# One transfer instead of two for the tokens of a block, and another order of ScalarE's conversions, in a Fourier and two-layer kernel on Trainium2

## The chip, the cores and the metric

The kernel runs on 1 core of one Trainium2 chip. The metric is the device time of one execution in microseconds (us). Engines are named as in the profile: PE (matmul), PEld (its weight loads), DVE (VectorE), ACT (ScalarE), POOL (GpSimd), SP (SyncE, which here only issues transfers).

## What is computed

Three stages follow each other (shapes: batch 4, sequence 3072, width 256):

```python
X = np.fft.fft(np.fft.fft(x, axis=1), axis=2).real          # Fourier stage, (4, 3072, 256)
h = X @ moe_w_in                                             # width 2048
y = np.where(h > 0, h, np.exp(np.minimum(h, 0)) - 1) @ moe_w_out
h = np.maximum(y @ moe2_w_in, 0); u, v = h[..., :512], h[..., 512:]
vn = (v - mean(v)) / sqrt(var(v) + 1e-6)
out = (u * (einsum('ts,bsd->btd', w_spatial, vn) + b)) @ moe2_w_out
```

## The kernel before, in words

The order of work on every engine is the order of the program text; only semaphores hold an engine back. Float32 products are made of three matmuls of a high and a low part (`matmul3`, L186 to L191), so most operands are split into two tiles: ACT rounds (`copy`, L164), then DVE or POOL subtracts (L165).

**Fourier stage** (L239 to L480). Twelve slots (four batches, three parts of the sequence) of folding on DVE and matmuls on PE. Its results are written to DRAM as `a` (16 blocks of 128 x 2 x 384 or 386, one for each batch b and token class c) by `evac` (L357); ACT copies them out of PSUM, and for the last batch ACT also issues the store. Beside this, weights that arrive as 64-bit floats are converted to float32: `late_load(n)` (POOL issues a transfer of 512 KB into a tile `wbits`), `late_begin(n)` (two passes on ACT: `mag`, and `cvr`, the rest), `late_end(n)` (six operations on DVE, which also issues the load of n + 2) and `late_keep(n)` (POOL issues a store of `cvr` into the tile `big`). Twelve such weights are converted in all: 0 to 4 at the end of the Fourier stage, 5 and 6 while `moe_w_in` is multiplied by the Fourier matrix (`pw`, L535 to L557), the rest in the first steps of the next stage. Two `wbits` tiles and a few `cv` tiles are used in turn, so a conversion can wait for an earlier one's store.

**Middle stage** (L567 to L840), both layers of the first perceptron and the first of the second. The 16 blocks of tokens follow each other, with eight steps each (a step is two of the sixteen slices of the 2048 units). A step s runs `s1` (the slice's products `pe` and `po`), `combine` on DVE, an ELU on ACT and DVE, and three steps later `s2`, which accumulates the second product in four PSUM banks `acc`. After the last step of a block `evac_x2` splits the four banks, and 14 *pieces* are put on a list: six `v_piece` (normalised on POOL and DVE, stored by SP and added up in DRAM by accumulating POOL transfers `v<-v`) and eight `u_piece` (L740). They run one or two at a time in the next block's steps: the last two `u` pieces at the end of step 7, the first `v` and `u` of the new list at the start of the step after it. A `u_piece` is six matmuls into a PSUM bank `pu`, a ReLU on ACT into one of three SBUF tiles in turn (L754, L755), and a store to DRAM that SP issues (L756); ACT can write a tile again only when its store three pieces ago has landed. The banks of `pe`, `po`, `pv`, `pu` are four in turn.

The tokens of a block are loaded by `load_x` (L501): half 0 of `a` (128 rows of 1536 or 1544 bytes, L504), half 1 without its row 0 (127 rows, L505), and row 0 of the middle column, broadcast to 128 rows (`xmid`, L508). Row 0 of half 1 must be zero: POOL clears it once before the first block (L523), and as the tile `xraw` is one and the same, no load touches that row. `split_x` (L511) rounds on ACT and subtracts on POOL. In the main loop the load for the block after the next step group is issued at the end of step g = 1 (L836, from block 1 on), and split at g = 4.

**Last stage** (from L842), the product with the 3072 x 3072 matrix, 1400 us, not touched.

Of the kernel before, what the change touches and what calls it, by code (L numbers as in the profile page):

```python
# [9 lines left out]
F32 = mybir.dt.float32  # L10
F32R = mybir.dt.float32r
U32 = mybir.dt.uint32
# [3 lines left out]
P = 128  # L16
B, S, D = 4, 3072, 256
# [5 lines left out]
TC = 512  # L23
NCH = S // TC
ND = 129
EVE = 386
# [36 lines left out]
def chunk_n(c):  # L63
    return EVE if c == 0 else ODD
# [67 lines left out]
def fourier_ffn_gated_kernel(ctx: ExitStack, tc: tile.TileContext, t, out: bass.AP):  # L132
    nc = tc.nc
# [28 lines left out]
    def split(hi, lo, src, engine=None):  # L162

        nc.scalar.copy(hi, src)  # L164
        (engine or nc.vector).tensor_tensor(lo, src, hi.bitcast(F32), op=ALU.subtract)  # L165
# [30 lines left out]
    late_at, late_raw, late_weights = {}, {}, []  # L196
    EARLY = 5

    def late_load(n):
        if n < len(late):  # L200
            name, at, _ = late[n]
            late_at[n] = [wr.tile([P, 2, D, 2], U32, tag="bits", bufs=2, name="wbits")]
            nc.gpsimd.dma_start(late_at[n][0], t[name][at])

    def late_begin(n, mag=None):
# [6 lines left out]
    def late_end(n, **k):  # L212
        if n < len(late):
            bits, mag = late_at.pop(n)
            num = wr.tile([P, 2 * D], U32, tag="cv1", name="cv1")
            f64_end(late_raw[n], bits.rearrange("p a d w -> p (a d) w"), mag, num, late_raw[n], **k)
            late_load(n + 2)

    def late_halves(n):
        _, at, dst = late[n]  # L220
# [18 lines left out]
    with ExitStack() as ph:  # L239
# [21 lines left out]
        def load_q(b, i):  # L261
            if b not in qs:
                home, tag = (big_p, f"big{b - 1}") if b in (1, 2) else (qp, "q")
                qs[b] = home.tile([P, 3, 4, 4, ND], F32, tag=tag, name=f"q{b}")
            nc.sync.dma_start(qs[b][:, i], t["xq"][b, :, i])
# [137 lines left out]
        load_bits(2)  # L403
        load_rows384(1)
        load_q(1, 0)
        def load_dt():
            nc.sync.dma_start(raw_dt, t["dt"])

# [9 lines left out]
        for k in range(SLOTS):  # L418
            b, i = divmod(k, 3)
            if done and (k in PACE or k == SLOTS - 1):  # L420
                w1_high(done - 1)
            fold(b, i)
            if i == 0:
                row0(b)
            mid_columns(b, i)
            if b and i == 0:
                for c in CLASSES:
                    evac(b - 1, c)
            if i == 2:
                keep_mids(b)  # L430
            for c in CLASSES:
                for z in range(2):
                    group(b, c, z, i)
            if k in PACE:
                if done:
                    w1_low(done - 1)
                else:
                    w1_begin(0)
                w1_end(done)
                load_bits(done + 3)  # L440
                done += 1
                w1_begin(done)
            for f, *a in loads.get(k, []):
                f(*a)
            if k == SLOTS - 1:
                w1_low(done - 1)
            if k == 4:
                nc.scalar.copy(halves_dt, raw_dt)
            if k == SLOTS - 3:
                late_load(0)  # L450
                late_load(1)
                big = [big_p.tile([P, 12 * TC], F32R, tag=f"big{x}", name=f"big{x}") for x in range(2)]
                late_weights.append([x[:, : NF1 * D].rearrange("p (f d) -> p f d", f=NF1) for x in big])
            if k == SLOTS - 2:
                late_begin(0, cvp.tile([P, TC], U32, tag="mag", name="mag"))

        row_sums = {}
        mid_rows = xop.tile([B, 2, EVE], F32, tag="mid_rows", bufs=1, name="mid_rows")

# [5 lines left out]
        def evac_rows(c):  # L465
# [1 line left out]
            nc.scalar.dma_start(m_d[c], mid_rows[:, c, : chunk_n(c)])  # L467

        beside = {
            0: [(evac, B - 1, 2)],  # L470
            1: [(evac, B - 1, 3)],
            2: [(sum_rows, 0), (evac, B - 1, 0), (evac, B - 1, 1), (sum_rows, 1)],
            3: [(evac_rows, 0), (evac_rows, 1)],
        }
        for n in range(EARLY):
            late_end(n)
            late_keep(n)
            late_begin(n + 1, cvp.tile([P, TC], U32, tag="mag", name="mag") if n < EARLY - 1 else None)
            for f, *a in beside.get(n, []):
                f(*a)  # L480

# [10 lines left out]
    wo1, weo = late_weights[0], [[x[:, NF1 * D :] for x in big], [wp.tile([P, DFF1], F32R, name=f"wo{h}") for h in "hl"]]  # L492
    wmid = wp.tile([P, NF1], F32, name="wmid")

    nh = vp.tile([P, 1], F32, name="nh", bufs=1)
    nc.gpsimd.memset(nh, -0.5)

    blocks = [(b, c) for b in range(B) for c in range(4)]
    xt = {}

    def load_x(i):  # L501
        b, c = blocks[i]
        n = chunk_n(c)
        nc.sync.dma_start(xraw[:, 0, :n], a_d[b][c][:, 0])  # L504
        nc.sync.dma_start(xraw[1:, 1, :n], a_d[b][c][1:, 1])  # L505
        m = xp.tile([P, EVE], F32, tag="xmid", bufs=2, name=f"xmid{i}")
        src = m_d[c][b] if c < 2 else a_d[b][c][0, 1]
        nc.sync.dma_start(m[:, :n], src.partition_broadcast(P))  # L508
        xt[i] = m

    def split_x(i):  # L511
        m = xt[i]
        n = chunk_n(blocks[i][1])
        hi = xp.tile([P, 2, EVE], F32R, tag="xhi", bufs=2, name=f"xhi{i}")
        lo = xp.tile([P, 2, EVE], F32R, tag="xlo", bufs=2, name=f"xlo{i}")
        split(hi[:, :, :n], lo[:, :, :n], xraw[:, :, :n], nc.gpsimd if i else None)
        xt[i] = (hi, lo, m)

    def load_wmid(q):
        nc.sync.dma_start(wmid[:, 4 * q : 4 * q + 4], wm_d[q].rearrange("o (f p) -> p (o f)", p=P))  # L520

    xraw = xp.tile([P, 2, EVE], F32, tag="xraw", name="xraw")
    nc.gpsimd.memset(xraw[:1, 1], 0.0)  # L523
    load_x(0)
    split_x(0)
    load_x(1)
    with tc.tile_pool(name="w1p", bufs=2, reuse_waits="tile", side="right") as w1p:
        row = None

        def mid_row(q, acc):  # L530
            x = w1p.tile([1, TC], F32, tag="mid_row", name="mid_row")
            nc.scalar.copy(x, acc[:1])
            nc.scalar.dma_start(wm_d[q], x)

        for q in range(DFF1 // TC):  # L535
            s = slice(q * TC, (q + 1) * TC)
            pieces = [w1_piece(2 * q + kt) for kt in range(2)]
            sums = [pp.tile([P, TC], F32, tag="pp", name=f"pw{z}") for z in range(2)]
            for z in range(2):
                for kt in range(2):  # L540
                    matmul3(
                        sums[z],
                        [x[:, kt, z * P : (z + 1) * P] for x in dt],
                        pieces[kt],
                        kt == 0,
                        kt == 1,
                    )
            for z in range(2):
                split(*(x[:, s] for x in weo[z]), sums[z])
            if row is not None:  # L550
                mid_row(*row)
            row = q, sums[1]
            if q % 2 == 0:
                n = EARLY + q // 2
                late_end(n)
                late_keep(n)
                late_begin(n + 1)  # L557
        mid_row(*row)
# [217 lines left out]
    def run_norms(n=None):  # L776
# [7 lines left out]
            nm()  # L784
        del norms[:n]

    NG = len(groups)
    LAG = 3
    PIECES = (2, 2, 2, 2, 1, 2, 1, 2)
    for s in range(NG + LAG):  # L790
        new = s < NG
        tail = s - LAG
        step = groups[tail][1] if tail >= 0 else -1
        if 0 <= s - 2 < NG:
            dve_g(s - 2)
        if 0 <= s - 1 < NG:
            act_neg(s - 1)
        if new:
            pe, po = s1(s, 0)
            combine(s, 0, pe, po)  # L800
        n = s + EARLY
        late_low(n - 1)
        late_end(n)
        late_keep(n)
        if step == 0:
            run_pieces(PIECES[0])
        if tail >= 0:
            s2(tail, 0)
        if new and groups[s][0] == 1:
            split_wo1(groups[s][1])  # L810
        if 0 <= s - 2 < NG and not plain(s - 2):
            act_hi(s - 2)
            dve_lo(s - 2)
        if 0 <= s - 1 < NG:
            act_exp(s - 1)
        late_begin(n + 1)
        late_high(n)
        if new:
            pe, po = s1(s, 1)
            combine(s, 1, pe, po)  # L820
        run_norms()
        run_sums(2)
        if tail >= 0:
            s2(tail, 1)
        if step == 7:
            evac_x2(groups[tail][0])
        if 1 <= step <= 7:
            run_pieces(PIECES[step])
        if step == 7:
            i = groups[tail][0]  # L830
            u = [("u", i, j, h) for j in range(4) for h in range(2)]
            for k in range(6):
                pieces += [("v", i, k), u.pop(0)]
            pieces += u
        if new and groups[s][0] < len(blocks) - 1:
            if groups[s][1] == 1 and groups[s][0]:  # L836
                load_x(groups[s][0] + 1)
            if groups[s][1] == 4:
                split_x(groups[s][0] + 1)
    ffn_early.close()  # L840
# [390 lines left out]
```

## Time and profile before

| | |
|---|---|
| median of 3 runs | 2814.07 us (2811.02 to 2817.68) |
| the profiled execution | 2814.41 us, span 2812.6 us |
| busy share of the span | PE 96%, PEld 83%, DVE 74%, ACT 46%, POOL 18% |
| mean granted TensorE clock | 0.979 of full |
| middle stage, 280 to 1235 us: PE busy | 874.4 of 955 us |

The span runs from the first to the last instruction of the program; the execution's own time is 1.8 us more. Busy shares are means over three stages with different limits, so the stretches are to be read one by one. A clock of 1.00 is 2.4 GHz, 0.50 is 1.2 GHz.

### The profile page before, as it was taken

How to read it: one execution, taken by the hardware profiler on the slowest of the kernel's cores; microseconds unless marked ns; L12 is line 12 of the kernel's file. 1: busy time of each engine (PE TensorE's matmuls, PEld its weight loads, DVE VectorE, ACT ScalarE, POOL GpSimd, SP SyncE). 2: the span in 40 equal slices, each digit the busy share in tenths (PEclk: the TensorE clock that was granted, in tenths of full speed). 3: DMA queues.
4: the chain of work that ended last, by engine and by line, in shares of the span. 5: the costliest groups of instructions: out<-in, count | busy, mean ns of one | idle time of the engine just before them, and what ended most of it. 6: DMA issues, size and time to landing. Idle time of an engine off the chain costs nothing.

```text
span 2812.6 us, 34540 instructions
## 1 busy us (share of the span) xinstructions
PE 2686.9 (96%) x12588; PEld 2328.8 (83%) x12588; DVE 2072.2 (74%) x2541; ACT 1288.8 (46%) x1709; POOL 495.5 (18%) x909
## 2 busy tenths in 40 slices
PE   8889989988889999989899999999999999999999
PEld 4559989988879899989788888888888888888877
DVE  9799777777777787777577766776966577676775
ACT  3457666666656667666332332323333233322332
POOL 0102233343441243434202010000000000000000
PEclk9999999999999999999999999999999999999999
DMA  9412465556664565656969789787856777677683
GB/s 375 141 35 108 132 128 142 126 129 132 122 118 159 141 142 136 125 121 139 292 239 334 251 274 302 252 279 251 308 209 236 246 260 254 232 266 276 225 288 111
DMA packets 212654, 565.01 MB, mean 201 GB/s; under 512 B 24952, under 2 KB 50553, under 8 KB 210948
## 3 DMA queue, kind: packets, MB, share of 16 engines
q1 hardware_dynamic: 165598, 460.53, 46.1%
q0 software_dynamic: 45888, 100.68, 19.4%
q8 instruction: 98, 1.61, 0.2%
q10 hardware_dynamic: 998, 1.61, 0.2%
q14 instruction: 72, 0.59, 0.1%
HBM read 397.01 MB, written 171.48 MB: 202 GB/s over the span
## 4 chain that ended last, share of the span: by engine, by line
PE 80%; DVE 8%; DMA 5%; ACT 3%; SPq 1%; issue 1%; POOL 0%; DVEq 0%; ACTq 0%; POOLq 0%
PE a L190 17%; PE a L191 17%; PE a L189 17%; PE acc L189 5%; PE acc L191 4%; PE acc L190 4%; DMA u<-uu 4%; PE pa L345 2%; DVE glo L637 2%; PE po L189 1%; PE pv L189 1%; PE pv L190 1%; PE po L190 1%; PE po L191 1%; PE pv L191 1%
## 5 line engine op out<-in xcount | busy, mean ns | idle before, releaser
L191 PE MATMUL a<-whi,vlo 128*128 128x512 f32 x1920 | 747.5, 389 | 0.0
L190 PE MATMUL a<-wlo,vhi 128*128 128x512 f32 x1920 | 747.3, 389 | 0.0
L189 PE MATMUL a<-whi,vhi 128*128 128x512 f32 x1920 | 747.0, 389 | 0.0
L910 ACT CAST whi<-raw 128x1024 fp32r<-128x1024 f32 x240 | 252.5, 1053 | 808.8 <-PE a L191 415.9
L916 DVE TENSOR_TENSOR wlo<-raw,whi 128x1024 fp32r<-128x1024 f32 x240 | 293.7, 1224 | 369.0 <-ACT whi L910 368.8
L190 PEld LDWEIGHTS a<-wlo,vhi 128*128 128x128 f32 x1920 | 360.4, 188 | 75.3
L189 PEld LDWEIGHTS a<-whi,vhi 128*128 128x128 f32 x1920 | 360.4, 188 | 75.2
L191 PEld LDWEIGHTS a<-whi,vlo 128*128 128x128 f32 x1920 | 360.3, 188 | 75.0
L637 DVE TENSOR_TENSOR glo<-h,ghi 128x1536 fp32r<-128x1536 f32 (+1 forms) x120 | 224.2, 1869 | 228.4 <-ACT ghi L632 228.4
L189 PE MATMUL acc<-ghi,big 128*128 128x384 f32 (+1 forms) x960 | 333.7, 348 | 0.0
L191 PE MATMUL acc<-ghi,big 128*128 128x384 f32 (+1 forms) x960 | 331.9, 346 | 0.0
L190 PE MATMUL acc<-glo,big 128*128 128x384 f32 (+1 forms) x960 | 331.2, 345 | 0.0
L900 DVE TENSOR_TENSOR raw<-raw 128x1024 f32<-128x1024 f32 x240 | 294.2, 1226 | 10.9 <-DMA raw<-in_wT 7.6
L955 POOL DMA_DIRECT2D u<-u x32 | 25.7, 834 | 1112.0 <-DVE sum L972 668.8
L608 ACT ACTIVATE e<-h 128x1536 f32<-128x1536 f32 (+1 forms) x128 | 190.0, 1484 | 55.0 <-DVE h L600 55.0
L773 POOL DMA_DIRECT2D v<-v x226 | 203.2, 1262 | 49.9 <-DVE v L727 37.4
L622 DVE SCALAR_TENSOR_TENSOR h<-e,h 128x1536 f32<-128x1536 f32 (+1 forms) x120 | 210.4, 1753 | 0.0
L613 ACT ACTIVATE e<-e 128x1536 f32<-128x1536 f32 (+1 forms) x128 | 190.4, 1487 | 0.2
L190 PEld LDWEIGHTS acc<-glo,big 128*128 128x128 f32 x960 | 188.0, 196 | 0.2
L189 PEld LDWEIGHTS acc<-ghi,big 128*128 128x128 f32 x960 | 187.5, 195 | 0.1
L191 PEld LDWEIGHTS acc<-ghi,big 128*128 128x128 f32 x960 | 186.8, 195 | 0.0
L632 ACT CAST ghi<-h 128x1536 fp32r<-128x1536 f32 (+1 forms) x120 | 176.3, 1469 | 21.5 <-DVE h L622 21.2
(166 smaller groups left out, 4183.2 us busy)
## 6 DMA issues: line engine op xcount, KB each, us to landing
raw<-in_wT SPq DMA_DIRECT2D x480, 512.0 KB
vlo<-v SPq DMA_DIRECT2D x120, 512.0 KB
v<-v POOLq DMA_DIRECT2D x226, 256.0 KB, 5.9
v<-v SPq DMA_DIRECT2D x224, 256.0 KB
u<-uu SPq DMA_DIRECT2D x128, 192.0 KB
u<-u POOLq DMA_DIRECT2D x16, 1024.0 KB, 8.6
q<-in_xq SPq DMA_DIRECT2D x12, 1032.0 KB
out<-sum SPq DMA_DIRECT2D x48, 256.0 KB
```

The source lines that it names most:

```text
L189: nc.tensor.matmul(acc, lhsT=w[0], rhs=x[0], start=start, stop=False, skip_group_check=more)
L190: nc.tensor.matmul(acc, lhsT=w[0], rhs=x[1], start=False, stop=False, skip_group_check=more)
L191: nc.tensor.matmul(acc, lhsT=w[1], rhs=x[0], start=False, stop=stop, skip_group_check=more)
L608: nc.scalar.activation(e[:, :, :w], st[s]["h"][:, :, :w], AF.Relu, scale=-1.0)
L613: nc.scalar.activation(e[:, :, :w], e[:, :, :w], AF.Exp, scale=-1.0)
L622: nc.vector.scalar_tensor_tensor(out=g[:, :, :w], in0=e[:, :, :w], scalar=-1.0, in1=h[:, :, :w], op0=ALU.add, op1=ALU.max)
L632: nc.scalar.copy(st[s]["hi"][:, :, :w], st[s]["h"][:, :, :w])
L637: nc.vector.tensor_tensor(st[s]["lo"][:, :, :w], st[s]["h"][:, :, :w], st[s]["hi"][:, :, :w].bitcast(F32), op=ALU.subtract)
L773: nc.gpsimd.dma_start(dst, v, accum_op=ALU.add)
L900: nc.vector.tensor_tensor(res, total, y, op=ALU.add if sg > 0 else ALU.subtract)
L910: nc.scalar.copy(hi, total)
L916: nc.vector.tensor_tensor(lo, total, hi.bitcast(F32), op=ALU.subtract)
```

## The change

`load_x` takes a new tile for each block and loads both halves of `a` with one transfer of 128 rows. A new `clear_x` lets POOL set row 0 of half 1 to zero behind the load, before `split_x`; in the main loop it stands at the end of step g = 2. At the end of the Fourier stage weights 2 and 3 are loaded into the three `bits` tiles of the pool `cvp` earlier (their loads no longer wait for `late_end(0)` and `late_end(1)`, which now load 4 and 5), and ACT's conversions stand elsewhere in its order: 1 and 2 ahead of the last batch's copies, 3 and 4 between them, 5 behind the rounding of the first `pw`. The tile `nh` is allocated and set later.

```diff
-    def late_load(n):
+    def late_load(n, home=wr, bufs=2):
...
-            late_load(n + 2)
+            if n not in (2, 3):
+                late_load(n + (4 if n < 2 else 2))
...
             if k == SLOTS - 2:
-                late_begin(0, cvp.tile([P, TC], U32, tag="mag", name="mag"))
+                late_load(2, cvp, 3)
+                early_begin(0)
+
+        late_load(3, cvp, 3)
...
         beside = {
-            0: [(evac, B - 1, 2)],
-            1: [(evac, B - 1, 3)],
-            2: [(sum_rows, 0), (evac, B - 1, 0), (evac, B - 1, 1), (sum_rows, 1)],
+            0: [(early_begin, 1), (early_begin, 2), (evac, B - 1, 2)],
+            1: [(evac, B - 1, 3), (early_begin, 3)],
+            2: [(sum_rows, 0), (evac, B - 1, 0), (evac, B - 1, 1), (sum_rows, 1), (early_begin, 4)],
             3: [(evac_rows, 0), (evac_rows, 1)],
         }
         for n in range(EARLY):
             late_end(n)
             late_keep(n)
-            late_begin(n + 1, cvp.tile([P, TC], U32, tag="mag", name="mag") if n < EARLY - 1 else None)
...
-        nc.sync.dma_start(xraw[:, 0, :n], a_d[b][c][:, 0])
-        nc.sync.dma_start(xraw[1:, 1, :n], a_d[b][c][1:, 1])
+        raw = xp.tile([P, 2, EVE], F32, tag="xraw", name=f"xraw{i}")
+        nc.sync.dma_start(raw[:, :, :n], a_d[b][c])
...
+    def clear_x(i):
+        nc.gpsimd.memset(xt[i][0][:1, 1, : chunk_n(blocks[i][1])], 0.0)
...
-    xraw = xp.tile([P, 2, EVE], F32, tag="xraw", name="xraw")
-    nc.gpsimd.memset(xraw[:1, 1], 0.0)
     load_x(0)
+    clear_x(0)
     split_x(0)
...
                 n = EARLY + q // 2
+                if q == 0:
+                    late_begin(n)
                 late_end(n)
...
             if groups[s][1] == 1 and groups[s][0]:
                 load_x(groups[s][0] + 1)
+            if groups[s][1] == 2:
+                clear_x(groups[s][0] + 1)
             if groups[s][1] == 4:
                 split_x(groups[s][0] + 1)
```

## Rows read from the trace of the kernel before

**Rows 1.** The page: busy time of each engine in us, share of the span, instructions.

```profile
PE 2686.9 (96%) x12588; PEld 2328.8 (83%) x12588; DVE 2072.2 (74%) x2541; ACT 1288.8 (46%) x1709; POOL 495.5 (18%) x909
```

**Rows 2.** Stretches: length, busy us of PE, PEld, DVE, ACT, POOL, clock, DMA share, GB/s.

```profile
280.00:1235.00 955.00, 874.40 (x4663) 847.62 (x4662) 722.74 (x930) 621.89 (x843) 345.13 (x647) 0.96 0.58 131
...
908.00:978.00 70.00, 69.17 (x372) 67.29 (x372) 56.77 (x74) 49.23 (x67) 23.30 (x49) 0.98 0.57 142
```

**Rows 3.** Waits, 280 to 1235 us: who for whom, us in all, times, longest.

```profile
ACT uu L755 <- DMA u<-uu: 105.0, 13, 12.6
...
PE po L189 <- ACT uu L755: 77.4, 13, 10.5
```

**Rows 4.** Timeline of SP, 640 to 720 us: start, length, instruction.

```profile
655.12 0.35 SPq L505 DMA_DIRECT2D xraw<-a  x1
655.81 6.07 SPq L508 DMA_DIRECT2D xmid<-m  x1
...
666.80 9.22 SPq L756 DMA_DIRECT2D u<-uu  x3
```

**Rows 5.** Timeline of ACT and PE in the same boundary between blocks.

```profile
661.11 0.49 ACT L755 ACTIVATE uu<-pu 128x384 f32<-128x384 f32 x1 [0.21 <-PE pu L191]
...
675.18 0.49 ACT L755 ACTIVATE uu<-pu 128x384 f32<-128x384 f32 x1 [9.59 <-DMA u<-uu]
...
675.73 0.69 PE L189 MATMUL po<-xhi,woh 128*128 128x384 f32 x1 [7.47 <-ACT uu L755]
```

**Rows 6.** Stretches at that boundary, columns as in the second group.

```profile
656.00:662.00 6.00, 6.00 (x36) 6.00 (x35) 5.79 (x10) 4.86 (x7) 1.77 (x2) 1.00 1.11 222
...
670.00:674.00 4.00, 0.00 (x0) 0.00 (x0) 0.00 (x0) 0.00 (x0) 0.00 (x0) 0.93 0.07 25
```

**Rows 7.** Timeline of SP, 178 to 200 us.

```profile
181.76 0.29 SPq L505 DMA_DIRECT2D xraw<-a  x1
196.59 0.35 SPq L508 DMA_DIRECT2D xmid<-a  x1
```

**Rows 8.** Stretches behind those transfers, columns as in the second group.

```profile
187.00:189.00 2.00, 2.00 (x11) 1.60 (x10) 2.00 (x2) 1.97 (x2) 0.00 (x0) 1.00 0.07 25
...
193.00:196.00 3.00, 3.00 (x13) 2.06 (x12) 2.21 (x5) 1.88 (x2) 0.00 (x0) 1.00 0.00 0
...
198.00:200.00 2.00, 2.00 (x11) 1.60 (x10) 0.86 (x1) 2.00 (x3) 0.00 (x0) 1.00 0.22 68
```

**Rows 9.** Line 505, 270 to 1235 us: ns min/median/max of an issue, first and last start.

```profile
L505 SPq DMA_DIRECT2D xraw<-a x13: 278/344/730, 281.2 to 1189.5; - x13
```

**Rows 10.** Timeline of ACT at the last boundary between blocks.

```profile
1274.01 0.49 ACT L755 ACTIVATE uu<-pu 128x384 f32<-128x384 f32 x1 [0.21 <-PE pu L191]
...
1278.58 0.49 ACT L755 ACTIVATE uu<-pu 128x384 f32<-128x384 f32 x1
```

**Rows 11.** First and last of 13 stretches of 8 us, each from where PE resumes.

```profile
297.00:305.00 8.00, 8.00 (x37) 8.00 (x38) 5.87 (x7) 5.22 (x6) 2.99 (x6) 0.79 0.23 84
...
1210.30:1218.30 8.00, 8.00 (x31) 8.00 (x32) 5.87 (x7) 5.21 (x6) 4.77 (x8) 0.64 0.23 83
```

**Rows 12.** Timeline, end of the Fourier stage; idle time before and its releaser in brackets.

```profile
113.22 0.67 ACT L170 ACTIVATE mag<-wbits 128x512 f32<-128x512 f32 x1 [1.43 <-DMA wbits<-in_moe_w_out]
...
118.37 0.41 POOL L523 MEMSET xraw<- 1x386 f32 x1
...
119.65 0.66 ACT L170 ACTIVATE cv<-wbits 128x512 f32<-128x512 f32 x1 [3.53 <-DMA big<-cvr]
...
120.76 0.83 ACT L164 CAST xhi<-xraw 128x772 fp32r<-128x772 f32 x1
```

**Rows 13.** The chain that ended last, first piece on PE behind it.

```profile
184.69 0.45 PE po L189
```

**Rows 14.** Timeline of POOL behind the load of a block.

```profile
676.47 0.19 POOL L719 TENSOR_SCALAR ve<-sums 128x1 f32<-128x1 f32 x1 [18.69 <-ACT sq L718]
```

**Rows 15.** Transfers issued in 654 to 676 us: times, KB each, median us to landing.

```profile
v<-v POOLq DMA_DIRECT2D x4, 256.0 KB, 8.5
```

More of the change, by code (lines that the diff above doesn't have):

```diff
@@ L197, in fourier_ffn_gated_kernel @@
     EARLY = 5
-    def late_load(n):
+    def late_load(n, home=wr, bufs=2):
         if n < len(late):
             name, at, _ = late[n]
-            late_at[n] = [wr.tile([P, 2, D, 2], U32, tag="bits", bufs=2, name="wbits")]
+            late_at[n] = [home.tile([P, 2, D, 2], U32, tag="bits", bufs=bufs, name="wbits")]
             nc.gpsimd.dma_start(late_at[n][0], t[name][at])
@@ L405, in fourier_ffn_gated_kernel, with early_begin @@
         load_q(1, 0)
+        def early_begin(n):
+            late_begin(n, cvp.tile([P, TC], U32, tag="mag", name="mag"))
         def load_dt():
@@ L493, in fourier_ffn_gated_kernel @@
     wmid = wp.tile([P, NF1], F32, name="wmid")
-    nh = vp.tile([P, 1], F32, name="nh", bufs=1)
-    nc.gpsimd.memset(nh, -0.5)
     blocks = [(b, c) for b in range(B) for c in range(4)]
@@ L508, in load_x @@
         nc.sync.dma_start(m[:, :n], src.partition_broadcast(P))
-        xt[i] = m
+        xt[i] = (raw, m)
+    def clear_x(i):
+        nc.gpsimd.memset(xt[i][0][:1, 1, : chunk_n(blocks[i][1])], 0.0)
     def split_x(i):
-        m = xt[i]
+        raw, m = xt[i]
         n = chunk_n(blocks[i][1])
@@ L515, in split_x @@
         lo = xp.tile([P, 2, EVE], F32R, tag="xlo", bufs=2, name=f"xlo{i}")
-        split(hi[:, :, :n], lo[:, :, :n], xraw[:, :, :n], nc.gpsimd if i else None)
+        split(hi[:, :, :n], lo[:, :, :n], raw[:, :, :n], nc.gpsimd if i else None)
         xt[i] = (hi, lo, m)
@@ L785, in run_norms @@
         del norms[:n]
+    nh = vp.tile([P, 1], F32, name="nh", bufs=1)
+    nc.gpsimd.memset(nh, -0.5)
     NG = len(groups)
```

## The prediction

> **What bounds the kernel now.** I read the page first. PE is busy 96% of the span [rows 1], so a gain can only come from the stretches where it isn't. The last stage shows no such stretch and isn't touched; the middle one does: between 280 and 1235 us PE works 874.4 of 955 us while DVE and ACT have 722.7 and 621.9 us of work [rows 2], so none of the three is full.
>
> The view of waits for that stretch names nearly all of PE's loss in one line: 13 times PE's `po` waits for ACT's `uu`, 77.4 us in all, 10.5 us at most, and ACT's `uu` itself waited 13 times, 105.0 us, for the transfer `u<-uu` [rows 3]. So the thing to understand is a store of a `u` tile that lands late, 13 times. The loads of tokens in that stretch number 13 as well [rows 9].
>
> The timelines of one boundary between two blocks show the order. SP issues the second part of the token load at 655.12 us, right behind the first, and then sits 6.07 us in the issue of the broadcast `xmid`. The last two `u` tiles of the block are made by ACT from 661.11 us on, but SP gets to their stores only at 666.80 us [rows 4, 5]. The next `u` needs the first of these tiles back; ACT waits 9.59 us for it and PE 7.47 us for ACT [rows 5]. PE's stop is thus at 675.73 - 7.47 = 668.26 us.
>
> Why is the store late? The stretches show it. From 656 to 662 us the DMA engines are full (1.11), but from 670 to 674 us, with PE, DVE, ACT and POOL all idle, they are at 0.07 of their time and 25 GB/s [rows 6]. One engine of sixteen is 0.0625. A transfer is dripping through a single engine, and the stores stand behind it there. Which one? Two earlier spots hold the candidates apart. The two token transfers of another block are issued together, the second at 181.76 us, with nothing behind them for 15 us; from 187 to 189 us the DMA is again at 0.07 and 25 GB/s, and from 193 us on at 0. At 196.59 us the broadcast is issued alone: its issue takes 0.35 us, and it runs at 0.22 of all engines, 68 GB/s over 2 us [rows 7, 8]. So it isn't the broadcast that drips, though its issue takes 6.07 us where it follows the other two [rows 4]. What is left is one of the pair, and the pair differ in their rows: 128 and 127. At 25 GB/s a transfer of 127 x 1536 bytes takes 195,072 / 25,000 = 7.8 us, alone; two such transfers would take 15.6 us and would still drip from 193 to 196 us, where nothing moves [rows 8]. So only one of the pair drips, and I take it to be the one of 127 rows.
>
> The last boundary is the counter-test: no token load is issued there, `uu` is written at 1274.01 and again into the reused tile at 1278.58 us with no wait shown [rows 10].
>
> **The change, part by part.** *The load in one transfer of 128 rows.* It removes the dripping transfer; 13 stalls of 77.4 us in all [rows 3] lose their cause. With each stall goes a loss of clock: in the 8 us after PE resumes the mean granted clock is 0.79 in the first of the 13 and 0.64 in the last [rows 11], although PE had run at 1.00 before it stopped. Over the 13 windows the missing part of the clock adds up to 3.31, that is 8 x 3.31 = 26.5 us of work at full speed (about 2 us for each stall, 4 us at 1.2 GHz instead of 2.4 GHz). Together 103.9 us. One SP issue less for each block (0.35 us there [rows 4]) is on a queue that sets nothing once it isn't held up: 0.
>
> What is next late where the stall was? The store of the last but one `u` tile still has to land in time. From its `uu` at 661.11 us to PE's stop at 668.26 us are 7.15 us; less the two passes of 0.49 us the store has 6.2 us [rows 5]. At the last boundary it was back within 1278.58 - 1274.01 - 0.49 = 4.1 us [rows 10]: no stall. With POOL's accumulating transfers under way it is slower; those of 256 KB took 8.5 us in this very stretch [rows 15], and a store of 192 KB that took as long would be 8.5 - 6.2 = 2.3 us too late. The bounds of what is left are so 0 and 13 x (2.3 + 2.0 of clock) = 56 us. The accumulating ones run in a few boundaries only up to that moment, and the token load, now spread, is issued some 6 us ahead of the store; I take 3 us in all, near the row of the last boundary.
>
> The Trainium skill's page "DMA: Bandwidth & Descriptors" has two rules that bear on this. Its section "Anatomy of one DMA — SWDGE (gpsimd) path" gives about 2.0 us plus bytes over 436 GB/s per transfer, whatever its rows, fitted on transfers of GpSimd: by that the 127 rows would take 2.4 us, nothing would drip, and the edit would be worth nothing. The trace disagrees (25 GB/s at 0.07 of the engines, for over 5 us). Its section "Why a DMA increments its semaphore by 16 and not by 1" says that the number of engines divides the slowest dimension, one for 127 rows and sixteen for 128; the trace agrees with the first half, and the whole 103.9 us hang on the second.
>
> *`clear_x` on POOL.* 15 more memsets like the one of 0.41 us [rows 12]. Each also waits for the token load, and behind it in POOL's queue stand the small operations of the next `v` piece (L719 to L724), then DVE's normalisation and the stores that follow. Cover: POOL idles 18.69 us before L719 there [rows 14], of which about 7.5 us belong to PE's stall; 11 us are left. Cost 0 while the load lands within about 11 us of its issue; without any cover 15 x 0.41 = 6 us, plus whatever the load is late.
>
> *The end of the Fourier stage.* ACT waited 1.43 us for the load of a weight and 3.53 us for a store out of a `cv` tile, then did conversion 5 (0.66 us and as much again) and only then rounded the first tokens at 120.76 us [rows 12]. From there a chain of DVE work runs to 184.69 us, where PE takes over [rows 13], so a shift of the rounding shifts PE. After the change loads 2 and 3 come early, and conversion 5 stands behind the rounding; what holds the rounding then is the memset, at 118.37 + 0.41 = 118.78 us, behind the fifth conversion's store, which moves forward by the 1.43 us: 117.35 us. Gain 120.76 - 117.35 = 3.4 us. Bounds: 0, if the fifth conversion is held by the last copies of the Fourier stage as before, and 1.43 + 3.53 + 1.3 = 6.3 us. The loads only change places in POOL's queue; `nh` later: 0.
>
> **Sum**, against the profiled execution's own 2814.4 us (0.3 us over the median): 2814.4 - 77.4 - 26.5 - 3.4 + 3 = 2710 us.
>
> **The rivals.** *The stores stay late (2.3 us a boundary).* Same bytes, and DMA already full from 656 to 662 us [rows 6]; against it the last boundary. Then 2814.4 - 107.3 + 56 = 2763 us. *Another engine becomes the bound.* DVE's 722.7 us in 955 - 104 = 851 us are 85% and its chains are serial; if each block lost 3 us to it, 13 x 3 = 39 us, 2746 us. Against it: from 908 to 978 us, between two stalls, PE is busy 69.17 of 70 us, and DVE has 56.8 us of work [rows 2]. *The change doesn't do it,* since something other than the 127 rows drips (the broadcast, say, when it stands behind a load): the Fourier end alone, 2811 us. Rows 7 and 8 speak against it. *Slower, by the memset.* Each load that lands later than 11 us after its issue holds POOL, with it DVE's normalisation, and in the end PE. Before, the drip lasted till about 674 us, 19 us after the issue; a load that took 20 us would cost 9 us at each boundary, and above 107 / 13 = 8.3 us the kernel is slower: at 12 us late 13 x 12 - 107 = 49 us more, 2863 us. It needs the new load to be slower than the old one.
>
> **How the numbers follow.** Chances: forecast 0.82, with its own range 2698 (Fourier end at its upper bound, no remaining wait, and a clock that gives back a little more) to 2725 us; stores late 0.09; DVE 0.04; no effect 0.03; slower 0.02. The range reaches up halfway into the second and third case: 2698 to 2745 us. A change of less than 0.2% (5.6 us) can't be told from none on this kernel. Faster 0.95, same 0.03 (the case without effect is 0.1% off), slower 0.02.
>
> **What would show it.** Right: no line `PE po <- ACT uu` above 10 us in the waits of the middle stage; the broadcast's issues at 0.4 us; no stretch at 0.07 DMA share with all engines idle; a clock of 0.99 or more from 200 to 1130 us; the first `xhi` near 117.4 us. Wrong in size: `ACT uu <- DMA u<-uu` still there with waits of some 2 us; PE waiting for DVE's `q` or `h` several times per block. Wrong in kind: a memset with microseconds of idle time before it and DVE waiting for POOL behind it, or the drip still there at 25 GB/s.

## The result

| | before | after |
|---|---|---|
| median of the runs beside each other | 2814.9 us | 2720.5 us (2719.4 to 2722.7) |
| ratio, 95% interval | | 0.9667 [0.965, 0.9683] |
| span of the profiled execution | 2812.6 us | 2718.4 us |
| mean granted clock | 0.979 | 0.994 |

The kernel became 3.3% faster; 2710 us were forecast and 2698 to 2745 as the range. Three stretches, cut at the first `pv` and the last `pe` matmul so that each holds the same matmuls in both kernels, show where the 94.2 us of the span came from. The columns are those of [rows 2]; first the kernel before, then the changed one.

```profile
0.00:221.80 221.80, 192.67 (x624) 119.08 (x625) 192.21 (x313) 96.46 (x175) 14.46 (x27) 0.95 0.47 175
221.80:1313.80 1092.00, 1011.40 (x5417) 981.26 (x5417) 841.11 (x1081) 723.50 (x981) 393.85 (x752) 0.96 0.57 132
1313.80:2812.60 1498.80, 1482.87 (x6550) 1228.50 (x6548) 1038.86 (x1148) 468.85 (x555) 87.20 (x131) 1.00 0.75 255
```

```profile
0.00:219.00 219.00, 191.69 (x624) 118.66 (x625) 192.11 (x313) 96.70 (x175) 15.47 (x29) 0.96 0.48 177
219.00:1219.00 1000.00, 989.28 (x5418) 956.78 (x5417) 845.29 (x1081) 723.89 (x981) 402.68 (x765) 1.00 0.63 144
1219.00:2718.40 1499.40, 1483.13 (x6550) 1228.75 (x6548) 1038.75 (x1148) 468.94 (x555) 87.70 (x131) 0.99 0.75 255
```

The head is 2.8 us shorter, the middle 92.0 us, the tail 0.6 us longer. In the middle PE's idle time fell from 1092.0 - 1011.4 = 80.6 to 10.7 us, and its busy time by 22.1 us for the same matmuls, while the clock of that stretch went from 0.96 to 1.00. The waits of PE there, changed kernel (who for whom, us in all, times, longest), against 77.4 us in 13 waits [rows 3]:

```profile
PE po L189 <- ACT uu L761: 6.0, 7, 1.5
PE po L189 <- DVE h L606: 4.1, 13, 0.3
PE pe L189 <- DVE q L599: 0.3, 2, 0.2
```

ACT's own wait for the stores did not go away. It fell from 105.0 us in 13 waits [rows 3] to 24.3 us in 11, 2.2 us each:

```profile
ACT uu L761 <- DMA u<-uu: 24.3, 11, 3.6
```

The same boundary between two blocks, on SP of the changed kernel (against [rows 4]):

```profile
621.24 0.42 SPq L507 DMA_DIRECT2D xraw<-a  x1
621.72 0.49 SPq L510 DMA_DIRECT2D xmid<-m  x1
622.30 1.76 SPq L787 DMA_DIRECT2D v<-v  x2
628.23 7.16 SPq L762 DMA_DIRECT2D u<-uu  x3
```

The broadcast now takes 0.49 us to issue, not 6.07, and SP reaches the first `u` store at 628.23 us, right behind the pass that made the tile. ACT and POOL there (against [rows 5, 14]):

```profile
627.71 0.49 ACT L761 ACTIVATE uu<-pu 128x384 f32<-128x384 f32 x1 [0.21 <-PE pu L191]
...
634.55 0.49 ACT L761 ACTIVATE uu<-pu 128x384 f32<-128x384 f32 x1 [2.35 <-DMA u<-uu]
```

```profile
627.86 0.41 POOL L514 MEMSET xraw<- 1x386 f32 x1 [3.49 <-DMA xraw<-a]
635.83 0.19 POOL L725 TENSOR_SCALAR ve<-sums 128x1 f32<-128x1 f32 x1 [7.56 <-ACT sq L724]
```

ACT still waits 2.35 us for the store, where it waited 9.59 us. PE, which works on other products meanwhile, waits 0.24 us where it waited 7.47 us:

```profile
635.09 0.45 PE L189 MATMUL po<-xhi,woh 128*128 128x384 f32 x1 [0.24 <-ACT uu L761]
```

POOL waits 3.49 us for the load, and then another 7.56 us for ACT, so its memset holds up nothing here. The stretches at that spot (against [rows 6]):

```profile
630.00:632.00 2.00, 2.00 (x12) 1.77 (x11) 2.00 (x2) 1.32 (x4) 0.00 (x0) 1.00 1.11 262
632.00:634.00 2.00, 2.00 (x14) 2.00 (x13) 1.13 (x3) 0.20 (x1) 0.00 (x0) 1.00 1.06 275
634.00:636.00 2.00, 1.75 (x10) 1.44 (x10) 0.00 (x0) 1.45 (x4) 0.17 (x1) 1.00 0.14 51
```

No drip at 0.07 is left; instead all DMA engines are full until 634 us, and ACT goes on right behind that, at 634.55 us.

### The profile page after: what moved, and what is told of

It is laid out like the page before. It is cut to its first block, busy times and chain, and to the rows that moved or that the text cites. A ratio compares the mean times of both kernels' runs of the same rounds, so it can differ in the third digit from the quotient of the medians.

```text
span 2718.4 us, 34530 instructions
## 1 busy us (share of the span) xinstructions
PE 2664.1 (98%) x12588; PEld 2304.2 (85%) x12588; DVE 2076.1 (76%) x2541; ACT 1289.5 (47%) x1709; POOL 505.8 (19%) x924
## 4 chain that ended last, share of the span: by engine, by line
PE 89%; DVE 6%; DMA 3%; ACT 2%; issue 1%; DVEq 0%; ACTq 0%; SPq 0%
PE a L190 17%; PE a L191 17%; PE a L189 17%; PE acc L191 6%; PE acc L189 6%; PE acc L190 5%; PE pa L346 3%; DMA u<-uu 2%; PE po L189 2%; PE po L190 1%; PE po L191 1%; PE pv L189 1%; PE pv L190 1%; PE pv L191 1%; PE pu L189 1%; PE pu L191 1%
## 5 line engine op out<-in xcount | busy, mean ns | idle before, releaser
L189 PE MATMUL acc<-ghi,big 128*128 128x384 f32 (+1 forms) x960 | 325.1, 339 | 0.0
L191 PE MATMUL acc<-ghi,big 128*128 128x384 f32 (+1 forms) x960 | 324.8, 338 | 0.0
L190 PE MATMUL acc<-glo,big 128*128 128x384 f32 (+1 forms) x960 | 323.7, 337 | 0.0
L638 ACT CAST ghi<-h 128x1536 fp32r<-128x1536 f32 (+1 forms) x120 | 176.4, 1470 | 22.1 <-DVE h L628 21.2
L190 PEld LDWEIGHTS acc<-glo,big 128*128 128x128 f32 x960 | 181.5, 189 | 0.5
L189 PEld LDWEIGHTS acc<-ghi,big 128*128 128x128 f32 x960 | 181.0, 189 | 0.1
L191 PEld LDWEIGHTS acc<-ghi,big 128*128 128x128 f32 x960 | 180.9, 188 | 0.0
```

What stands on the lines that cost most here:

```text
L189: nc.tensor.matmul(acc, lhsT=w[0], rhs=x[0], start=start, stop=False, skip_group_check=more)
L190: nc.tensor.matmul(acc, lhsT=w[0], rhs=x[1], start=False, stop=False, skip_group_check=more)
L191: nc.tensor.matmul(acc, lhsT=w[1], rhs=x[0], start=False, stop=stop, skip_group_check=more)
L638: nc.scalar.copy(st[s]["hi"][:, :, :w], st[s]["h"][:, :, :w])
```

## The experiments

**Two transfers of 128 rows.** Is it the rows, or that there is one transfer less?

```diff
-        nc.sync.dma_start(raw[:, :, :n], a_d[b][c])
+        for z in range(2):
+            nc.sync.dma_start(raw[:, z, :n], a_d[b][c][:, z])
```

> The changed kernel, but the tokens of a block come in two transfers of 128 rows each, half 0 and half 1, with the memset behind them. Theory (127 rows go through one DMA engine, the number of transfers is nothing): as the changed kernel, 2718 to 2723 us; PE waits for ACT's uu about 6 us in all; the broadcast's issue stays under 1 us. Rival (one transfer instead of two is what helps, by one issue less on SP and one less completion to wait for): a good part of the loss comes back, 2760 us or more.

Measured: 2718.65 us (2716.7 to 2720.2), span 2717.1, PE's waits for `uu` 6.7 us in 7, the broadcast's issues 0.4 to 1.1 us. So it isn't that there is one transfer less; what is left of the edit is the rows.

**The old load put back** in the changed kernel (one tile, 128 and 127 rows, one memset before the loop).

```diff
-        raw = xp.tile([P, 2, EVE], F32, tag="xraw", name=f"xraw{i}")
-        nc.sync.dma_start(raw[:, :, :n], a_d[b][c])
+        raw = xraw
+        nc.sync.dma_start(raw[:, 0, :n], a_d[b][c][:, 0])
+        nc.sync.dma_start(raw[1:, 1, :n], a_d[b][c][1:, 1])
...
```

> The changed kernel with the old load alone put back: 128 and 127 rows, one tile, one memset at the start; the new order of the Fourier stage stays. Theory (the 127 rows make the 13 stalls; the Fourier part is worth 2.8 us): 2811 us, 13 waits of PE for ACT's uu of about 77 us in all. Rival (the new order of the Fourier stage gave part of the gain in the middle stage, since weights arrive and buffers come free earlier): 2780 us or less.

Measured: 2821.2 us, ratio to before 1.0022 [1.0012, 1.0031], span 2818.4 us. The stalls are all back, with the broadcast's issues at 3.1 to 12.5 us:

```profile
PE po L189 <- ACT uu L760: 79.3, 13, 9.1
```

But it came out 10 us above the expectation: the new Fourier order, which gained 2.8 us in the changed kernel, costs here. ACT's first rounding says why (timeline of ACT, run with the old load):

```profile
126.68 0.83 ACT L164 CAST xhi<-xraw 128x772 fp32r<-128x772 f32 x1 [10.54 <-DMA xraw<-a]
```

It waits 10.54 us for the tokens of block 0. SP's timeline of the same run shows the load leaving at 110.77 us; before the change its second part left at 89.92 us, where it had 30 us to land:

```profile
110.77 0.33 SPq L507 DMA_DIRECT2D xraw<-a  x1
111.14 0.41 SPq L508 DMA_DIRECT2D xraw<-a  x1
```

SP waited 23.0 us before that load, by the trace for DVE's L178, which ends at 110.69 us. L178 reads a weight's `wbits`, and the new order keeps those of weights 2 and 3 in `cvp`; that the tokens' tile takes over that memory is my reading.

**Only block 0 in 128 and 127 rows**, to test that.

```diff
-        nc.sync.dma_start(raw[:, :, :n], a_d[b][c])
+        if i:
+            nc.sync.dma_start(raw[:, :, :n], a_d[b][c])
+        else:
+            nc.sync.dma_start(raw[:, 0, :n], a_d[b][c][:, 0])
+            nc.sync.dma_start(raw[1:, 1, :n], a_d[b][c][1:, 1])
```

> The changed kernel, but only block 0 is loaded in 128 and 127 rows; all other blocks in one transfer. Theory (in the run with the old load put back, the first rounding waited 10.5 us for block 0 alone, because the new order lets that load go only at 111 us and its 127 rows then drip): the first xhi near 126.7 us instead of 118.0, the first u pass near 230.4 us, and the whole kernel 8 to 9 us slower than the changed one, 2727 to 2730 us. Rival (that delay came from the load of block 1 or from the broadcast): no more than 3 us slower, below 2724 us.

Measured: 2730.4 us (2727.0 to 2731.8), first rounding at 126.49 us after a wait of 10.38 us for the load, first `u` pass at 230.2 us. Theory held, with a median 0.4 us above its interval: in the new order one 127-row load, that of block 0, delays the rounding by 8.5 us and the whole kernel by 2730.4 - 2720.5 = 10 us.

**Row 0 left out, but in 112 and 15 rows.** As before the change, the first row isn't touched and no memset is needed in the loop.

```diff
...
+        nc.sync.dma_start(raw[1:113, 1, :n], a_d[b][c][1:113, 1])
+        nc.sync.dma_start(raw[113:, 1, :n], a_d[b][c][113:, 1])
...
```

> The changed kernel with half 1 loaded without its row 0, as before the change, but in two transfers: 112 rows and 15 rows; one tile, one memset at the start, three token transfers a block and no memset in the loop. Theory (a transfer is spread over as many engines as divide its rows, up to 16, so 112 go over 16 and 15 over 15): as the changed kernel or up to 3 us faster, 2716 to 2723 us, no stretch at 25 GB/s. Rival (a load that leaves out row 0, or a destination that does not begin at partition 0, is slow by itself): 2790 us or more.

Measured: 2716.0 us (2713.2 to 2717.0), PE's waits for `uu` 5.0 us in 6. So neither the missing row nor the start at another partition is slow; the count 127 is. No other slow count was tried. The Trainium skill's page "DMA: Bandwidth & Descriptors", section "Why a DMA increments its semaphore by 16 and not by 1", has the number of engines divide the rows, up to sixteen, and one for 127; the times of all four loads tried (127; 128; 112 with 15; 2 x 128) agree, though no run shows on how many engines the 15 rows went.

**Four `u` tiles in turn** in the changed kernel.

```diff
-        u = wr.tile([P, 2 * D], F32, tag=f"cv{1 + (2 * j + h) % 3}", name="uu")[:, :384]
+        u = wr.tile([P, 2 * D], F32, tag=f"cv{(1 + 2 * j + h) % 4}", name="uu")[:, :384]
...
-                sq = wr.tile([P, HV], F32, tag="cv0", name="sq")
+                sq = vp.tile([P, HV], mybir.dt.bfloat16, tag="sq", bufs=1, name="sq")
```

> The changed kernel with four u tiles in turn instead of three; the squares of which only the sum is used are written to a tile of bfloat16 of their own to make room. Theory (the 6.0 us that PE still waits for ACT's uu are the reuse of a tile whose store has not landed): these waits go, 6 us less in the span of the profile, 2713 to 2717 us. Rival (DVE or ACT is then late by as much): the line goes, PE waits for DVE instead, 2719 to 2722 us.

Measured: 2705.85 us (2705.1 to 2706.8), span 2703.5. The line `PE po <- ACT uu` is gone, and the gain is 14.9 us of span, more than twice the 6.0 us that the line showed and more than the theory's interval allows. The middle stretch with the same 5418 matmuls:

```profile
218.50:1205.50 987.00, 984.11 (x5418) 958.12 (x5417) 840.41 (x1081) 723.51 (x981) 399.61 (x765) 1.00 0.63 146
```

It is 13.0 us shorter: PE's idle time falls by 7.8 us (PE's waits for DVE too, from 4.4 to 2.6 us), its busy time by 5.2 us. The profile models the ends of overlapping matmuls, so a part of what a wait costs may stand in busy time; no run separates that. The squares' own tile is not the cause: their 90 passes take 715 ns in the median with the old tile and 714 ns with the new one, and the only engine that waits for them, POOL, does so about as long as before (427.0 and 434.6 us).

The edit does more than add a tile. A block has eight `u` pieces, and with three tiles the count starts anew in each block, so the tiles go 1 2 3 1 2 3 1 2 | 1 2 3: the first piece of a block takes back the tile of *two* pieces before, not of three, as the description of the kernel before has it. That is the store that stood behind the token load. With four tiles eight pieces come out even, and the tile is that of four pieces before. Three tiles counted on across blocks were not run; the tile wanted at the boundary of [rows 4] would then be one whose store SP issued just ahead of the load (kernel before):

```profile
654.23 0.32 SPq L756 DMA_DIRECT2D u<-uu  x1
```

> The changed kernel with four u tiles once more, beside the kernel before with four. Theory: 2704 to 2707 us, faster than the kernel before with four u tiles by the 2.8 us of the Fourier order and little else. Rival (the drip still costs in the kernel before with four tiles): the distance is 8 us or more.

Measured, the same kernel in another group of runs: 2706.3 us. `sq`, the squares that nobody reads (only their sum is used), moved to a small tile of its own, so that `cv0` became the fourth `u` tile.

**Four `u` tiles in the kernel before**, nothing else.

```diff
-        u = wr.tile([P, 2 * D], F32, tag=f"cv{1 + (2 * j + h) % 3}", name="uu")[:, :384]
+        u = wr.tile([P, 2 * D], F32, tag=f"cv{(1 + 2 * j + h) % 4}", name="uu")[:, :384]
```

(and `sq` moved as above).

> The kernel before, with its loads of 128 and 127 rows and its old Fourier order, and with nothing but four u tiles in turn (the squares go to a bfloat16 tile of their own). Theory (the 127 rows cost only because a u tile is wanted back while its store stands behind them; the u tile wanted at the boundary is now one whose store went out before the load): the waits of PE for ACT's uu go although the drip at 25 GB/s is still there, 2708 to 2714 us. Rival (the held-up queue also delays the stores of v, and with them DVE or ACT, so that most of the stalls come back elsewhere): 2730 us or more.

Measured: 2709.5 us (2707.1 to 2709.6), ratio 0.9620 [0.9606, 0.9635]. A fourth `u` tile, with the reuse that it makes even, gives more than the whole change. The first lines of PE's waits, the broadcast's issues (ns min/median/max), and the middle stretch:

```profile
PE po L189 <- DVE h L600: 2.0, 6, 0.3
PE pe L189 <- DVE q L593: 1.1, 1, 1.1
```

```profile
L508 SPq DMA_DIRECT2D xmid<-a x7: 3132/6480/13131, 280.9 to 1095.2; - x7
L508 SPq DMA_DIRECT2D xmid<-m x6: 4021/5266/11732, 348.7 to 960.4; - x6
```

```profile
221.50:1208.50 987.00, 983.70 (x5416) 957.64 (x5415) 840.59 (x1080) 723.38 (x981) 395.14 (x752) 1.00 0.63 146
```

The 127 rows still hold SP up for 3.1 to 13.1 us a block, but neither ACT nor PE waits for a store of `u` any more, and the middle stretch is 987.0 us, the same as with the new load and four tiles. The distance between the two kernels with four tiles is 3.2 us, about the 2.8 us of the Fourier order.

**The new load alone**, in the kernel before, with the old Fourier order.

```diff
-        nc.sync.dma_start(xraw[:, 0, :n], a_d[b][c][:, 0])
-        nc.sync.dma_start(xraw[1:, 1, :n], a_d[b][c][1:, 1])
+        raw = xp.tile([P, 2, EVE], F32, tag="xraw", name=f"xraw{i}")
+        nc.sync.dma_start(raw[:, :, :n], a_d[b][c])
...
+    def clear_x(i):
+        nc.gpsimd.memset(xt[i][0][:1, 1, : chunk_n(blocks[i][1])], 0.0)
...
```

> The kernel before with the new load alone: one transfer of 128 rows and the memset behind it; the Fourier stage keeps its old order. Theory (the load is worth all of the gain but the 2.8 us by which the new order brings the first u pass forward): first u pass near 224.4 us, 2721 to 2725 us. Rival (the new order is needed for more, since it also delays the first token load from 88 to 111 us): 2718 us or less, or above 2728 us.

Measured: 2722.9 us (2721.5 to 2724.7), first rounding at 120.36 us, span 3.0 us above the changed kernel. Theory held.

**No memset in the loop.** The kernel leaves row 0 of half 1 as it comes, from block 1 on.

```diff
-            if groups[s][1] == 2:
-                clear_x(groups[s][0] + 1)
```

> The changed kernel without the memsets in the loop (block 0 keeps its own), so that row 0 of half 1 holds what lies in memory and the result changes in that row. Theory (POOL's wait for the load, 71.9 us in 13 waits, lies in time in which POOL has nothing to do): 2716 to 2722 us, the same waits of PE for ACT's uu, 6 us. Rival (POOL's wait holds up the accumulating transfers and so the stores; this is what made the kernel with 112 and 15 rows 4 us faster): 2713 to 2716 us.

Measured: 2716.8 us (2714.7 to 2719.1), PE's waits for `uu` 6.6 us in 7. The median lies in the theory's interval, but the four times fall in two pairs, 2714.7 and 2719.0 us, one on each side. The memsets cost at most a few microseconds; whether they cost any stays open.

**Four `u` tiles, 112 and 15 rows**: the edits of these two runs together, in the changed kernel.

> The changed kernel with both edits that were faster: four u tiles in turn (the squares go to a bfloat16 tile of their own), and half 1 in 112 and 15 rows without a memset in the loop. Theory (with a fourth tile no store is waited for, so a load that lands sooner has nothing left to give; only the first memset of 0.4 to 0.9 us goes): 2703 to 2706 us, as with four tiles alone. Rival (the two gains add up): 2700 to 2702 us.

Measured: 2707.0 us (2706.9 to 2707.3): no gain over four tiles alone, as expected where no store is waited for any more, though 1 us above the theory's interval. The changed kernel with four tiles has the lowest median of all, 2705.9 us, but this one and the kernel before with four tiles are within 4 us of it.

## Why the prediction was right, and what was off

**The mechanism held.** The dripping transfer was the one of 127 rows; the stalls were stores of `u` behind it; they went, and the clock with them. The old load brings all 13 back, two loads of 128 do not, and 112 with 15 do not. What the prediction did not ask is why a tile is wanted back after two pieces; the runs with four tiles show that the late store costs nothing where the tile is wanted back after four.

**The size of the stalls held.** 103.9 us were read, 77.4 from the waits and 26.5 from the clock. The kernels in which `uu` waits for no store have a middle stretch of 987.0 us, 105.0 us below the 1092.0 of before. In the kernel before with four tiles the two parts come out singly: PE's idle time there is 987.0 - 983.7 = 3.3 us, 77.3 us less, and its busy time 1011.4 - 983.7 = 27.7 us less.

**The term that failed is what is left**: "I take 3 us in all". It is 1000.0 - 987.0 = 13.0 us (the middle stretch takes 996.9 to 1003.3 us in all runs with three tiles and no drip in the loop). The step took the last boundary as the nearest row, where a store was back within 4.1 us; but there no tokens are loaded. At a boundary with a load, the 386 KB of tokens and the broadcast stand ahead of the store beside the transfers of `v`, the DMA is full until 634 us, and the store asked for at 628.23 us let ACT go on at 634.55 us, just past the 6.2 us it had. That the load makes the difference is my reading; no run took it away. The upper bound of 56 us was too high, since PE waited in only 7 of 13 boundaries, 1.5 us at most, and the clock stayed at 1.00. The rival of the late stores was thus partly true, at a quarter of its price; its sign, ACT waiting some 2 us for `u<-uu`, did show, at 2.2 us in 11 waits, but most of each passes before PE needs the result.

**The Fourier stage** gave 2.8 us of the 3.4. In all runs, the first `pv` starts at 217.8 to 219.0 us with the new order (but for the two that load block 0 in 127 rows) and at 221.1 to 221.8 us with the old, so the 0.6 us that are missing are less than the scatter. The first rounding was held by the memset, as said, but at 117.98 us and not 117.35:

```profile
117.53 0.41 POOL L514 MEMSET xraw<- 1x386 f32 x1
117.98 0.84 ACT L164 CAST xhi<-xraw 128x772 fp32r<-128x772 f32 x1 [1.81 <-POOL xraw L514]
```

What the working did not see is that the new order holds the first load back until 111 us. With 128 rows it still lands in time; with 127 the order would have cost 6 us instead of gaining 2.8 (2818.4 - 2812.6 us of span, old load in both).

**`clear_x`** cost at most a few microseconds, as the run without its memsets shows: the load landed 7.3 us after its issue in the median and 10.6 us at most, inside the 11 us of cover.

**DVE** did not become the bound: 845.3 us of work in 1000 us, and with four tiles 840.4 in 987.0.

Of 10.1 us between the forecast and the measured span difference (104.3 and 94.2), 13.0 - 3 = 10 are the term that is left, 0.6 each the Fourier stage and the tail, and about 1 us goes the other way in the size of the stalls; only the first is clear of the scatter between runs.

## What to carry to other kernels

Where transfers drip at one sixteenth of the DMA with all engines idle, look at the number of rows, and see who stands behind the transfer in the queue. But ask first why anybody waits for that queue: here a fourth buffer was worth more than mending the transfer, and left 3.2 us between the kernels with the old load and the new, about what the Fourier order gives. Count, too, how many pieces lie between two uses of a buffer where a rotation starts anew. And a term for what remains should be taken from a row with the same traffic, not from the one spot where the traffic is absent.

## What the hardware showed that was not expected

A transfer that drips at 25 GB/s also holds up the engine that issues the next one: the broadcast behind it took 3.0 to 13.9 us to issue in the loop, 0.5 to 1.2 us without it. And the share of PE's loss that a view of waits names can be under half of what removing it gives: 6.0 us named, 13.0 us gained in that stretch, 7.8 of them idle time.
